# Partition maxima with one product, K^T V feature-major in two batches, and a new written-out order

## The chip, the cores and the metric

One core of a Trainium2 chip runs the whole program. It has TensorE (PE; its weight loads are listed as PEld), VectorE (DVE), ScalarE (ACT), GpSimd (POOL) and SyncE (SP), which issues all DMAs. The metric is the device time of one execution in microseconds (us), lower is better.

## What is computed

Random-feature attention, then two feed-forward layers on its 2304 tokens (4 batches of 576) of 512 columns (8 heads of 64):

```python
def phi(x):                                   # for q and k, scaled by 64 ** -0.25
    proj = np.einsum('bhsd,md->bhsm', x, omega)          # 128 features m
    h = proj - np.sum(x * x, axis=-1, keepdims=True) / 2.0
    return np.exp(h - np.max(h, axis=-1, keepdims=True)) / np.sqrt(m)
kv, z = einsum('bhsm,bhsd->bhmd', k_p, v), sum(k_p, axis=2)
x = einsum('bhsm,bhmd->bhsd', q_p, kv) / (einsum('bhsm,bhm->bhs', q_p, z)[..., None] + 1e-06)
x = x / sqrt(mean(x * x) + 1e-06) * rms_g                # layer 1, d_ff 1536
x = (silu(x @ w_gate) * (x @ w_val)) @ w_out
h = x @ w_in                                             # layer 2, d_ff 2048
out = where(h > 0, h, exp(min(h, 0)) - 1) @ w_out2
```

The weights arrive as 64-bit words and are made into float32 on the chip, then into two float16 planes (high and low part), so that a product of float32 accuracy is three float16 products.

## The kernel before, in words

*Work.* Attention is cut into 38 jobs, 20 of keys (four tiles of 128 tokens and one of 64 in each batch) and 18 of queries. Each job loads a tile, forms the features of all eight heads in two PSUM banks, takes maxima, and exponentiates (`phi`). Jobs 0 to 15 multiply in float32, the later ones in float16 planes (`SPLIT`). `NACT` says how many of a job's two banks ScalarE exponentiates head by head; the others are shifted by VectorE first. Key jobs add K^T V over the five tiles of a batch in two PSUM banks. For batches 0 and 1 (`KV32`) values and features stay float32: each product has the 65 columns of the values (64 and a column of ones) as stationary operand and the 128 features as moving operand, so the sum is [65 x 128] in each head, and `turned` scales it, splits it into planes, and turns it by products with the identity, to features on partitions. Batches 2 and 3 use float16 planes, with the features stationary. A query job multiplies its features with K^T V, divides, normalizes and lays out the token tile for layer 1.

The layers follow: `moe1_pair` and `moe1_out` by blocks of 256 tokens, then `moe2_quad` and `moe2_out`. Their products are the *spine*: they keep the order in which they are written. Meanwhile the weights are made: `conv_cols` and `conv_rows` call `Conv.words`, which on 128x1024 words forms the magnitude, the shifted low bits and the sign plane (0x8000 of the top half word), and `fp32`, which joins them.

*Maxima over partitions.* `spread(m, n)` takes n columns of values, one for each partition, turns them with a product (the columns stationary, the identity moving), lets VectorE reduce the n rows, and sends the maxima to all partitions with a second product with ones (n = 1), or with a diagonal (n > 1). It is called for the scale of each float16 attention job, of values, of each weight block, and at the end of each block of layer 1.

*Order.* The program is recorded as operations, and `Plan.order` simulates five engines with prices from `Plan.take` and waits from `Plan.wait`. It decides which operation each engine issues next, which engine takes an operation with several `ways`, and which PSUM bank (kind B) or large or middle tile (kinds L, M) a job gets. Spine operations have due times from `STRETCH`; others inherit them through their users with `INFL` and `LEAD`, shifted for each job by `BIAS`. `SPARE` and `BLIM` keep places free for the spine. Each engine then executes its list in order, and a waiting instruction holds all behind it. All instructions are issued in `play`, so they carry one line in the profile, L530; the tiles (arenas RX, RW, RA, RM, RS, RC, RI, RO and banks ps) tell them apart.

Of the kernel before, what the change touches and what calls it, by code (L numbers as in the profile page):

```python
# [17 lines left out]
P = 128  # L18
# [4 lines left out]
NACT, SPLIT = '12111011102010110100001022111212110111', '00000000000000001111111111111111111111'  # L23
# [116 lines left out]
class Plan:  # L140
# [4 lines left out]
    HOP = 0.14  # L145
    INTO, FROM = {"POOL": 0.19}, {"PE": 0.22, "POOL": 0.08}
    LAND, MARGIN = 1.7, 0.5
    SPAN = 3.4133
    SPARE = {"B": 2, "L": 2, "M": 2}
# [80 lines left out]
    def take(self, eng, real, fn, a, k):  # L230
# [23 lines left out]
        if eng == "PE":  # L254
            op.cost += 0.19 * (min(k["lhsT"].free_size(), n) < 64 and len(op.calls) == 1) + max(n, 64) / 2400.0 * (4 if k["rhs"].dtype == F32 else 1) + (0.0047 if k["rhs"].dtype == F32 else 0.0024)
        elif eng == "DVE":
            n = max(n, src.free_size()) if fn == "tensor_reduce" else n
            fast = fn in ("tensor_scalar", "tensor_copy", "memset") and "accum_out" not in k and src.space == bass.MemoryType.SB
            pair = "in1" in k and src.space == k["in1"].space == bass.MemoryType.SB
            op.both = pair or (fast and fn != "memset" and out.space == bass.MemoryType.SB and n > 1)  # L260
            op.cost += 0.068 + n / (1920.0 if fast else 960.0) + 0.0615 * vals + (0.3 if pair and n > 64 and out.partition_size() == 64 else 0.0)
        elif eng == "ACT":
            op.cost += (0.094 if src.space == bass.MemoryType.SB else 0.052) + n / 1200.0 + 0.093 * vals + (0.094 if "accum_out" in k else 0)
            op.cost += 0.12 if vals and out.partition_size() == 64 else 0.0
        elif eng == "POOL":
            op.cost += 0.088 * (len(op.calls) > 1)
            if fn == "tensor_scalar":
                op.cost += 0.066 + n / 980.0 if not vals else 0.243 + n / 1197.0 + 0.083 * (vals - 1)
            else:
                op.cost += 0.464 if n < 9 else 0.147 + n / (475.0 if aps["in1"].dtype == F32 else 530.0)  # L270
# [269 lines left out]
def fused(ctx: ExitStack, tc: tile.TileContext, qT, kT, kTt, qn, kn, v, v1, omT, eye, g, wg, wv, wo, w1, w2, out):  # L540
# [14 lines left out]
    RC = Arena(sb, "RC", 1216)  # L555
# [68 lines left out]
    RI = Arena(sb, "RI", 640)  # L624
    idn, ones, dg = RI.take([P], F16), RI.take([P], F16), RI.take([64], BF16)
    om, Wh, Wl = RO.take([P], F32), RO.take([P], F16), RO.take([P], F16)
    kap0 = tt([1])
    RS = Arena(sb, "RS", 2816)
# [8 lines left out]
    def spread(m, n, o=None):  # L637
# [14 lines left out]
        pe.matmul(out=o[:, 504:504 + n], lhsT=ones[0:n], rhs=r, start=True, stop=True)  # L652
        return o[:, 504:504 + n]
# [21 lines left out]
    class Conv:  # L675
# [15 lines left out]
        def words(self, st):  # L691
# [12 lines left out]
            vec.tensor_scalar(out=A16[:, :, 1], in0=r16[:, :, 3], scalar1=0x8000, scalar2=None, op0=ALU.bitwise_and)  # L704
# [124 lines left out]
    sv = tt([1])  # L829
# [12 lines left out]
    def setup_consts():  # L842
# [12 lines left out]
        vec.memset(ones, 1.0)  # L855
# [14 lines left out]
    def phi(load, n, key, pair=True):  # L870
# [28 lines left out]
        if split:  # L899
# [11 lines left out]
            iv, s, kap = sm(1, "qiv"), sm(1, "qs"), sm(1, "kap")  # L911
            vec.tensor_scalar(out=m_, in0=spread(m, 1), scalar1=1e-24, scalar2=None, op0=ALU.max)
            vec.tensor_scalar(out=iv.bitcast(I32), in0=m_.bitcast(I32), scalar1=1, scalar2=EXPM, op0=ALU.logical_shift_right, op1=ALU.bitwise_and)
            vec.tensor_scalar(out=sq[:n], in0=sq[:n], scalar1=0.0625, scalar2=None, op0=ALU.mult)
            vec.tensor_scalar(out=iv, in0=iv, scalar1=2.0 ** (64 - 12), scalar2=None, op0=ALU.mult)
            vec.reciprocal(out=s, in_=iv)
            vec.tensor_scalar(out=kap, in0=iv, scalar1=kap0, scalar2=None, op0=ALU.mult)
            Sx = S_r.next()
# [9 lines left out]
            vec.scalar_tensor_tensor(out=mx[:n], in0=mx[:n], scalar=kap[:n], in1=sq[:n], op0=ALU.mult, op1=ALU.subtract)  # L928
            vec.scalar_tensor_tensor(out=b[:n], in0=mx[:n], scalar=-LN2_14, in1=sq[:n], op0=ALU.add, op1=ALU.add)
            if nact:  # L930
                vec.tensor_scalar(out=nb[:n], in0=b[:n], scalar1=-1.0, scalar2=None, op0=ALU.mult)
            for i in range(2):
                if i < 2 - nact:
                    shifted(i, b, kap[:n], ALU.mult, ALU.subtract)
                else:
                    exps(i, kap[:n], nb)
        else:
# [35 lines left out]
    def values(b):  # L973
# [30 lines left out]

    def turned(b):

        kt = e_r.next()
        KV = kv_r[b % 2]
        for i in range(2):
            c = slice(512 * i, 512 * i + 512)  # L1010
            act.activation(out=kt[0:65, 0, c], in_=acc[i][0:65], func=AF.Copy, scale=sv[0:65])
            vec.scalar_tensor_tensor(out=kt[0:65, 1, c], in0=acc[i][0:65], scalar=sv[0:65], in1=kt[0:65, 0, c], op0=ALU.mult, op1=ALU.subtract)
        for a in range(2):
            for i in range(2):
                o = psP.next()
                with plan.group():
                    for h in range(4):
                        pe.matmul(out=o[:, h * 65:h * 65 + 65], lhsT=kt[0:65, a, (4 * i + h) * P:(4 * i + h) * P + P], rhs=idn[0:65, 0:65], start=True, stop=True)
                o = o[:, 0:260].rearrange("p (h c) -> p h c", h=4)
                if (a + i) % 2:  # L1020
                    vec.tensor_copy(out=KV[:, a, 4 * i:4 * i + 4, 0:65], in_=o)
                else:
                    act.activation(out=KV[:, a, 4 * i:4 * i + 4, 0:65], in_=o, func=AF.Copy)

    def k_job(b, t, key):
# [40 lines left out]
    def q_job(t, key):  # L1066
# [377 lines left out]
```

## Time and profile before

| | us |
|---|---|
| median of 3 runs | 977.3 (976.38 to 980.16) |
| span of the profiled execution (its time, no other is recorded) | 972.8 |
| TensorE busy | 911.0 |
| VectorE, GpSimd, ScalarE busy | 667.1, 599.8, 537.7 |

The span runs from the first to the last instruction. An engine's busy time is the union of its instructions. In lists by time a bracket gives the idle time of the engine before the instruction and what ended it. A float32 product appears as two records.

### The profile page before, as it was taken

The page shows a single profiled execution, that of the slowest core. Times are in us where ns is not written, and L with a number is a line of the kernel's source. Part 1 is how long each engine was busy: PE and PEld are TensorE (multiplying, and loading weights), DVE is VectorE, ACT ScalarE, POOL GpSimd, SP SyncE. Part 2 cuts the span into 40 slices and gives each one's busy share as a digit, 9 for nine tenths or more (in the row PEclk, how much of TensorE's full clock was granted, in tenths as well). Part 3 has the DMA queues.
Part 4 walks back from the last instruction along what each step waited for, and adds up shares of the span by engine and source line. Part 5 has one row for each costly group of instructions (what it writes and reads, how often), then busy time and mean ns, then how long its engine had stood idle before and what let it go on. Part 6 is the DMA issues. An engine that isn't in the chain of part 4 may idle for free. (4 is left out here: it accounts for less than half of the span.)

```text
span 972.8 us, 22167 instructions
## 1 busy us (share of the span) xinstructions
PE 911.0 (94%) x8904; PEld 802.7 (83%) x8904; DVE 667.1 (69%) x1570; ACT 537.7 (55%) x981; POOL 599.8 (62%) x617
## 2 busy tenths in 40 slices
PE   4486969999999999999999999999999999999998
PEld 4385858888888888888888888888888888888887
DVE  6988887867478585777866888777436565464642
ACT  5895554746455575584533557776435555255540
POOL 3668957967966788688573448996415265153540
PEclk9787989999999999999999999999999999999999
DMA  9765645033511442116674433000000000000001
GB/s 288 209 189 161 173 141 168 7 77 89 131 45 33 88 94 63 37 45 172 196 218 135 142 125 123 31 2 6 18 18 17 12 13 12 17 18 12 12 13 44
DMA packets 82567, 82.57 MB, mean 85 GB/s; under 512 B 52896, under 2 KB 57888, under 8 KB 82464
## 3 DMA queue, kind: packets, MB, share of 16 engines
q1 hardware_dynamic: 82464, 81.16, 29.5%
q8 instruction: 69, 1.13, 0.5%
q14 instruction: 34, 0.28, 0.1%
HBM read 59.90 MB, written 8.91 MB: 71 GB/s over the span
## 5 line engine op out<-in xcount | busy, mean ns | idle before, releaser
L530 PEld LDWEIGHTS <-RW 128*128 128x128 f16 x4800 | 451.7, 98 | 69.0 <-issue 12.2
L530 PE MATMUL ps<-RM,RW 128*128 128x256 f16 (+1 forms) x3240 | 365.4, 271 | 5.0 <-ACT RA L530 3.1
L530 PEld LDWEIGHTS <-RA 128*128 128x128 f16 (+3 forms) x3128 | 261.0, 98 | 31.5 <-issue 1.8
L530 PE MATMUL ps<-RX,RA 128*128 128x256 f16 x1728 | 196.5, 273 | 1.2 <-DVE RM L530 1.2
L530 ACT ACTIVATE RM<-ps,RC 128x512 f32<-128x512 f32 (+1 forms) x135 | 90.0, 669 | 101.7 <-PE ps L530 67.1
L530 POOL TENSOR_TENSOR RA<-RA 64x512 f16<-64x512 f32 (+6 forms) x91 | 122.6, 1349 | 22.8 <-DVE RS L530 4.9
L530 POOL TENSOR_TENSOR RM<-RM 128x512 f16<-128x512 f32 (+1 forms) x94 | 100.9, 1077 | 42.0 <-ACT RM L530 36.2
L530 ACT ACTIVATE RM<-RM 128x512 f32<-128x512 f32 (+3 forms) x163 | 96.3, 592 | 43.9 <-DVE RM L530 39.5
L530 POOL TENSOR_SCALAR RM<-RM,RC 128x512 f32<-128x512 f32 x72 | 57.7, 802 | 93.6 <-ACT RM L530 93.5
L530 DVE SCALAR_TENSOR_TENSOR ps<-ps,RM 128x512 f32<-128x512 f32 x72 | 50.2, 697 | 83.3 <-POOL RM L530 83.3
L530 PE MATMUL ps<-RX,RW 128*128 128x256 f16 x864 | 98.4, 273 | 2.1 <-DMA RX<-RA 2.1
L530 DVE TENSOR_REDUCE RS<-ps 128x4 f32<-128x512 f32 (+5 forms) x146 | 75.4, 536 | 27.6 <-PE ps L530 26.9
L530 DVE SCALAR_TENSOR_TENSOR RM<-RM,ps 128x512 f32<-128x512 f32 x108 | 73.2, 681 | 26.8 <-ACT RM L530 17.9
L530 ACT ACTIVATE RA<-RA 128x1024 f32<-128x1024 f32 (+5 forms) x69 | 61.3, 897 | 49.8 <-DVE RA L530 12.8
L530 PE MATMUL ps<-RW,RA 128*128 128x256 f16 (+2 forms) x560 | 68.5, 276 | 6.1 <-ACT RW L530 4.9
L530 PE MATMUL ps<-RW 128*128 128x256 f16 x600 | 71.9, 273 | 0.9 <-DVE RM L530 0.9
L530 ACT ACTIVATE RA<-RA,RS 64x512 f16<-64x512 f32 (+3 forms) x69 | 51.7, 759 | 27.3 <-POOL RS L530 11.3
L530 POOL TENSOR_TENSOR RW<-RM,RW 128x256 f16<-128x256 f32 (+1 forms) x63 | 43.7, 704 | 34.4 <-ACT RW L530 18.5
L530 POOL TENSOR_SCALAR RA<-RA,RS 64x512 f32<-64x512 f32 (+2 forms) x63 | 43.9, 697 | 22.2 <-ACT RA L530 15.8
L530 POOL TENSOR_TENSOR RA<-RM,RA 128x256 f16<-128x256 f32 (+1 forms) x50 | 34.4, 696 | 32.1 <-ACT RA L530 21.0
L530 DVE SCALAR_TENSOR_TENSOR RM<-ps,RC,RM 128x256 f32<-128x256 f32 x54 | 25.1, 478 | 40.6 <-PE ps L530 40.5
L530 DVE TENSOR_TENSOR RM<-ps,RM 128x256 f32<-128x256 f32 x108 | 45.1, 420 | 9.8 <-ACT RM L530 6.6
(147 smaller groups left out, 1182.4 us busy)
## 6 DMA issues: line engine op xcount, KB each, us to landing
RA<-w SPq DMA_DIRECT2D x32, 512.0 KB, 4.0
RX<-wg SPq DMA_DIRECT2D x12, 512.0 KB, 5.2
RX<-wv SPq DMA_DIRECT2D x12, 512.0 KB, 6.2
RX<-wo SPq DMA_DIRECT2D x12, 512.0 KB, 4.3
out<-RM SPq DMA_DIRECT2D x36, 128.0 KB, 1.7
f<-RA SPq DMA_DIRECT2D x8, 512.0 KB, 3.7
RA<-f SPq DMA_DIRECT2D x8, 512.0 KB, 3.4
RA<-qn SPq DMA_DIRECT2D x11, 256.0 KB, 4.0
```

The costliest lines, as they stand in the source:

```text
L530: getattr(real, fn)(*[fix(x) for x in a], **{i: fix(x) for i, x in k.items()})
```

## The change

`spread` forms one product for each column, with the column repeated 128 times as stationary operand, so that each partition gets all 128 values, and VectorE's reduction gives the maximum on all partitions. K^T V of batches 0 and 1 has the features as stationary and the values as moving operand; `turned` is gone, and the sum is scaled and split straight from PSUM, values and ones apart. The sign plane may be made by VectorE, ScalarE or GpSimd. The shift by 14 log 2 is left out for batches 0 and 1, and some small steps of `phi`, `values` and the denominator are joined. Squares of float16 jobs are always ScalarE's. The tables of the planner and its prices are replaced.

```diff
-NACT = '12111011102010110100001022111212110111'
+NACT = '12111011102010120100001022111212100111'
-AHEAD, BLIM = 2665473.472, 7
+AHEAD, BLIM = 2665473.472, 8
-FINE = 9
+FINE = 8
-BIAS = [0, -24, -6, -13, 9, 11, 1, -18, 4, 16, 26, 0, 3, 0, -42, -66, 48, 0, 24, -36, 11, -47, 60, -76, -82, 71, 3, 7, -74, -72, 7, -40, -68, -29, 214, -138, -2, -19, 6, 12, -10, -26, 30, 98, 29, -5, -6, 50, -58, 0, -29, 29, 0, 7, -28, 113, -9, 8, -23, 3, 1, 0]
+BIAS = [-48, -21, 9, 2, -1, -5, -19, -32, 7, -5, 23, 66, -12, -19, -40, -65, 96, 8, 86, -57, -31, -96, 87, -725, -93, 90, -8, -57, -521, 77, -106, 90, -388, -166, 245, -985, -415, -1104, 9, -61, 181, -50, -534, 1233, 108, -310, 475, -14, -96, 271, -73, 840, 77, 90, 285, 988, 70, 890, -200, 25, -589, -195]
-LOOK, WEIGH = 0.076, 80
-PRICE = [2.61, 1.246, 0.912, 2.233, 0.537, 1.098]
+LOOK, WEIGH = 0.0, 80
+PRICE = [2.241, 0.976, 0.79, 0.283, 0.288, 0.28]
-INFL, LEAD = 1.815, 51.617
-STRETCH = (11.046, 890.942, 0.188)
+INFL, LEAD = 1.963, 51.66
+STRETCH = (2.134, 3.532, 0.08)
-    SPARE = {"B": 2, "L": 2, "M": 2}
+    SPARE = {"B": 2, "L": 1, "M": 2}
...
-        o = bank.next() if o is None else o
         top = m.bitcast(BF16).rearrange("p (n w) -> p n w", w=2)[:, :, 1]
-        pe.matmul(out=o[0:n, 0:P], lhsT=top, rhs=idn, start=True, stop=True)
-        if n == 1:
-            r = sm(1, "spr").bitcast(BF16)[0:1, 0:1]
-            vec.tensor_reduce(out=r, in_=o[0:1, 0:P], op=ALU.max, axis=AX.X)
-        else:
-            c = sm(1, "spc")
-            r = dg[0:n, 0:n]
-            vec.tensor_reduce(out=c[0:n], in_=o[0:n, 0:P], op=ALU.max, axis=AX.X)
-            vec.tensor_scalar(out=r, in0=idn[0:n, 0:n], scalar1=c[0:n], scalar2=None, op0=ALU.mult)
-        pe.matmul(out=o[:, 504:504 + n], lhsT=ones[0:n], rhs=r, start=True, stop=True)
-        return o[:, 504:504 + n]
+        r = sm(n, "spr")
+        for i in range(0, n, 4):
+            k = min(4, n - i)
+            o = bank.next()
+            with plan.group():
+                for j in range(k):
+                    pe.matmul(out=o[:, j * P:j * P + P], lhsT=top[:, i + j:i + j + 1].to_broadcast([P, P]), rhs=idn, start=True, stop=True)
+            vec.tensor_reduce(out=r[:, i:i + k], in_=o[:, 0:k * P].rearrange("p (n k) -> p n k", n=k), op=ALU.max, axis=AX.X)
+        return r
...
-            vec.tensor_scalar(out=A16[:, :, 1], in0=r16[:, :, 3], scalar1=0x8000, scalar2=None, op0=ALU.bitwise_and)
+            h, o = r[:, :, 1].bitcast(F32), A16[:, :, 1].bitcast(F16)
+            plan.choose(lambda: vec.tensor_scalar(out=A16[:, :, 1], in0=r16[:, :, 3], scalar1=0x8000, scalar2=None, op0=ALU.bitwise_and),
+                        lambda: act.activation(out=o, in_=h, func=AF.Copy, scale=2.0 ** -100),
+                        lambda: pool.tensor_scalar(out=o, in0=h, scalar1=2.0 ** -100, scalar2=1.0, op0=ALU.mult, op1=ALU.mult))
...
-            if nact:
+            top = LN2_14 if pair else 0.0
+            if not pair:
+                nb = mx
+            elif nact:
                 vec.tensor_scalar(out=nb[:n], in0=mx[:n], scalar1=LN2_14, scalar2=None, op0=ALU.add)
...
-                    pe.matmul(out=acc[h // 4][0:65, (h % 4) * P:(h % 4) * P + P], lhsT=V32[:n, t, h], rhs=e[:n, h * P:(h + 1) * P], start=first and h % 4 == 0, stop=last and h % 4 == 3)
+                    pe.matmul(out=acc[h // 4][:, (h % 4) * 65:(h % 4) * 65 + 65], lhsT=e[:n, h * P:(h + 1) * P], rhs=V32[:n, t, h], start=first and h % 4 == 0, stop=last and h % 4 == 3)
             if last:
-                turned(b)
+                KV = kv_r[b % 2]
+                for i in range(2):
+                    a = acc[i][:, 0:260].rearrange("p (h c) -> p h c", h=4)
+                    hi, lo = KV[:, 0, 4 * i:4 * i + 4], KV[:, 1, 4 * i:4 * i + 4]
+                    for c, f in ((slice(0, 64), sv[:, b:b + 1]), (slice(64, 65), 2.0 ** 6)):
+                        act.activation(out=hi[:, :, c], in_=a[:, :, c], func=AF.Copy, scale=f)
+                        vec.scalar_tensor_tensor(out=lo[:, :, c], in0=a[:, :, c], scalar=f, in1=hi[:, :, c], op0=ALU.mult, op1=ALU.subtract)
...
         for i in range(2):
-            vec.tensor_scalar(out=rc[:, 4 * i:4 * i + 4].unsqueeze(2), in0=a4[i][:, :, 64:65], scalar1=128e-6 * 2.0 ** 20, scalar2=None, op0=ALU.add)
+            for a, m, b in runs:
+                vec.tensor_scalar(out=rc[a:a + m, 4 * i:4 * i + 4].unsqueeze(2), in0=a4[i][a:a + m, :, 64:65], scalar1=128e-6 * 2.0 ** 20, scalar2=ivs[a:a + m, b:b + 1], op0=ALU.add, op1=ALU.mult)
         vec.reciprocal(out=rc, in_=rc)
-        for a, m, b in runs:
-            vec.tensor_scalar(out=rc[a:a + m], in0=rc[a:a + m], scalar1=ivs[a:a + m, b:b + 1], scalar2=None, op0=ALU.mult)
```

## Rows read from the trace of the kernel before

**Rows 1.** Stretches: length, busy (instructions) of each engine, clock, DMA share, GB/s

```profile
0.00:51.50 51.50, 22.51 (x160) 19.70 (x161) 40.13 (x99) 36.60 (x54) 27.96 (x30) 0.89 0.83 235
51.50:72.70 21.20, 20.96 (x218) 20.02 (x217) 18.72 (x37) 19.96 (x45) 13.91 (x12) 0.87 0.77 213
72.70:88.80 16.10, 6.61 (x74) 5.14 (x74) 14.41 (x50) 10.58 (x23) 12.97 (x15) 0.65 0.44 138
88.80:121.00 32.20, 31.97 (x348) 29.97 (x346) 27.53 (x51) 15.46 (x25) 29.67 (x28) 0.96 0.65 182
121.00:160.00 39.00, 29.85 (x267) 25.36 (x267) 29.98 (x67) 20.26 (x28) 27.02 (x25) 0.87 0.46 147
160.00:972.80 812.80, 799.14 (x7843) 702.47 (x7841) 536.32 (x1270) 434.85 (x808) 488.22 (x512) 1.00 0.23 64
```

**Rows 2.** Waits of TensorE from 0 to 160 us: total, times, longest

```profile
PE ps L530 <- DVE RS L530: 15.0, 7, 6.0
```

**Rows 3.** Order of time, all engines, 137 to 148 us: start, length, what

```profile
137.36 0.22 PE L530 MATMUL ps<-RI,RS 128*1 128x128 f16 x1
...
141.95 1.22 DVE L530 TENSOR_SCALAR_CACHE_REDUCE RW<-RW 128x1024 f32<-128x1024 f32 x1 [1.09 <-ACT RW L530]
...
143.28 0.27 DVE L530 TENSOR_REDUCE RS<-ps 1x1 bf16<-1x128 f32 x1
...
143.60 0.16 PE L530 MATMUL ps<-RS,RI 1*128 1x1 bf16 x1 [6.03 <-DVE RS L530]
...
143.83 4.45 PE L530 MATMUL ps<-RM,RW 128*128 128x256 f16 x20
```

**Rows 4.** Order of time on TensorE alone, behind 143 us

```profile
143.83 22.48 PE L530 MATMUL ps<-RM,RW 128*128 128x256 f16 x180
...
196.43 0.22 PE L530 MATMUL ps<-RI,RS 128*1 128x128 f16 x1
196.57 2.79 PE L530 MATMUL ps<-RM,RW 128*128 128x256 f16 x24
...
440.75 0.16 PE L530 MATMUL ps<-RS,RI 1*128 1x1 bf16 x1 [0.33 <-DVE RS L530]
440.84 4.32 PE L530 MATMUL ps<-RM,RW 128*128 128x256 f16 x38
```

**Rows 5.** Second products of the maxima, whole span and behind 160 us

```profile
L530 PE MATMUL ps<-RS,RI 1*128 1x1 bf16 x44 | 7.5, 170 | 8.1 <-DVE RS L530 7.9
...
L530 PE MATMUL ps<-RS,RI x37: 158/172/173, 209.6 to 622.2; 1*128 1x1 bf16 x37
```

**Rows 6.** Order of time on TensorE, 58 to 77 us

```profile
58.67 7.29 PE L530 MATMUL ps<-RW,RA 128*65 128x128 f32 x64
...
68.52 0.88 PE L530 MATMUL ps<-RI,RW 65*128 65x65 f16 x20
...
71.08 0.90 PE L530 MATMUL ps<-RA,RW 128*128 128x65 f16 x24
...
76.91 0.22 PE L530 MATMUL ps<-RI,RS 128*2 128x128 f16 x1 [4.20 <-DVE RX L530]
```

**Rows 7.** Float32 weight loads by shape: busy, mean ns

```profile
L530 PEld LDWEIGHTS ps<-RO,RA 128*128 128x128 f32 x48 | 5.6, 192 | 0.0
...
L530 PEld LDWEIGHTS ps<-RO,RW 128*64 128x64 f32 x16 | 1.7, 137 | 0.0
```

**Rows 8.** Order of time on ScalarE, end of batch 0's K^T V

```profile
65.69 1.24 ACT L530 ACTIVATE RW<-ps,RC 65x512 f16<-65x512 f32 x2
...
69.30 0.67 ACT L530 ACTIVATE RA<-ps 128x260 f16<-128x260 f32 x2
```

**Rows 9.** VectorE's groups from 0 to 160 us: busy, mean ns

```profile
L530 DVE TENSOR_SCALAR RX<-RX 128x1024 uint16<-128x1024 uint16 x16 | 13.1, 821 | 3.4 <-POOL RX L530 3.4
...
L530 DVE TENSOR_SCALAR RS<-RS 128x8 f32<-128x8 f32 x10 | 4.8, 482 | 0.0
...
L530 DVE TENSOR_SCALAR RS<-ps 128x4 f32<-128x4 f32 x8 | 0.9, 148 | 0.0
```

More of the change, by code (lines that the diff above doesn't have):

```diff
@@ L145 @@
     HOP = 0.14
+    SAME = {"PE": 0.0, "DVE": 0.12, "ACT": 0.14, "POOL": 0.0, "SP": 0.06}
     INTO, FROM = {"POOL": 0.19}, {"PE": 0.22, "POOL": 0.08}
@@ L254, in take @@
         if eng == "PE":
-            op.cost += 0.19 * (min(k["lhsT"].free_size(), n) < 64 and len(op.calls) == 1) + max(n, 64) / 2400.0 * (4 if k["rhs"].dtype == F32 else 1) + (0.0047 if k["rhs"].dtype == F32 else 0.0024)
+            op.cost += 0.19 * (min(k["lhsT"].free_size(), n) < 64 and len(op.calls) == 1) + max(n, 64) / 2400.0 * (4 if k["rhs"].dtype == F32 else 1) + (0.0047 if k["rhs"].dtype == F32 else 0.0024) + (0.05 if k["rhs"].dtype == F32 and n < P else 0.0)
         elif eng == "DVE":
@@ L260, in take @@
             op.both = pair or (fast and fn != "memset" and out.space == bass.MemoryType.SB and n > 1)
-            op.cost += 0.068 + n / (1920.0 if fast else 960.0) + 0.0615 * vals + (0.3 if pair and n > 64 and out.partition_size() == 64 else 0.0)
+            tight = max([abs(y[-1][0]) for y in (src.ap, out.ap)]) == 1
+            op.cost += (0.01 if fn == "memset" and n < 9 else 0.068) + (0.0 if tight or not fast or n < 9 else 0.04) + (0.005 * n if fn == "reciprocal" else 0.0) + n / (1920.0 if fast else 960.0) + 0.0615 * vals + (0.3 if pair and n > 64 and out.partition_size() == 64 else 0.0)
         elif eng == "ACT":
             op.cost += (0.094 if src.space == bass.MemoryType.SB else 0.052) + n / 1200.0 + 0.093 * vals + (0.094 if "accum_out" in k else 0)
-            op.cost += 0.12 if vals and out.partition_size() == 64 else 0.0
+            op.cost += 0.12 if vals and out.partition_size() == 64 and src.space == bass.MemoryType.SB else 0.0
+            op.cost += 0.1 if src.space == bass.MemoryType.SB and src.ap[-1][0] != 1 and n > 8 else 0.0
         elif eng == "POOL":
@@ L267, in take @@
             if fn == "tensor_scalar":
-                op.cost += 0.066 + n / 980.0 if not vals else 0.243 + n / 1197.0 + 0.083 * (vals - 1)
+                op.cost += 0.27 if n < 9 else 0.186 + n / 980.0 if not vals else 0.243 + n / 1197.0 + 0.083 * (vals - 1)
             else:
-                op.cost += 0.464 if n < 9 else 0.147 + n / (475.0 if aps["in1"].dtype == F32 else 530.0)
+                op.cost += 0.53 if n < 9 else (0.1 if out.partition_size() == 64 and n < 1024 else 0.02) + 0.147 + n / (475.0 if aps["in1"].dtype == F32 else 530.0)
         else:
@@ L554, in fused @@
     RM = Arena(sb, "RM", 8192 + 24576 + 4096)
-    RC = Arena(sb, "RC", 1216)
+    RC = Arena(sb, "RC", 960)
     def tt(shape, dt=F32):
@@ L623, in fused @@
     RO = Arena(sb, "RO", 1024)
-    RI = Arena(sb, "RI", 640)
-    idn, ones, dg = RI.take([P], F16), RI.take([P], F16), RI.take([64], BF16)
+    RI = Arena(sb, "RI", 256)
+    idn = RI.take([P], F16)
     om, Wh, Wl = RO.take([P], F32), RO.take([P], F16), RO.take([P], F16)
     kap0 = tt([1])
-    RS = Arena(sb, "RS", 2816)
+    RS = Arena(sb, "RS", 2592)
     smalls = {}
@@ L910, in phi @@
             m_ = sm(1, "qma")
-            iv, s, kap = sm(1, "qiv"), sm(1, "qs"), sm(1, "kap")
-            vec.tensor_scalar(out=m_, in0=spread(m, 1), scalar1=1e-24, scalar2=None, op0=ALU.max)
+            iv, s, kap, kan = sm(1, "qiv"), sm(1, "qs"), sm(1, "kap"), sm(1, "kan")
+            vec.tensor_scalar(out=m_, in0=spread(m, 1), scalar1=1e-25, scalar2=None, op0=ALU.max)
             vec.tensor_scalar(out=iv.bitcast(I32), in0=m_.bitcast(I32), scalar1=1, scalar2=EXPM, op0=ALU.logical_shift_right, op1=ALU.bitwise_and)
-            vec.tensor_scalar(out=sq[:n], in0=sq[:n], scalar1=0.0625, scalar2=None, op0=ALU.mult)
-            vec.tensor_scalar(out=iv, in0=iv, scalar1=2.0 ** (64 - 12), scalar2=None, op0=ALU.mult)
+            vec.tensor_scalar(out=iv, in0=iv, scalar1=2.0 ** (66 - 12), scalar2=None, op0=ALU.mult)
             vec.reciprocal(out=s, in_=iv)
             vec.tensor_scalar(out=kap, in0=iv, scalar1=kap0, scalar2=None, op0=ALU.mult)
+            vec.tensor_scalar(out=kan, in0=iv, scalar1=kap0, scalar2=-1.0, op0=ALU.mult, op1=ALU.mult)
             Sx = S_r.next()
@@ L927, in phi @@
             maxima(False)
-            vec.scalar_tensor_tensor(out=mx[:n], in0=mx[:n], scalar=kap[:n], in1=sq[:n], op0=ALU.mult, op1=ALU.subtract)
-            vec.scalar_tensor_tensor(out=b[:n], in0=mx[:n], scalar=-LN2_14, in1=sq[:n], op0=ALU.add, op1=ALU.add)
-            if nact:
-                vec.tensor_scalar(out=nb[:n], in0=b[:n], scalar1=-1.0, scalar2=None, op0=ALU.mult)
+            vec.scalar_tensor_tensor(out=mx[:n], in0=mx[:n], scalar=kan[:n], in1=sq[:n], op0=ALU.mult, op1=ALU.add)
+            vec.scalar_tensor_tensor(out=nb[:n], in0=mx[:n], scalar=LN2_14, in1=sq[:n], op0=ALU.add, op1=ALU.subtract)
             for i in range(2):
                 if i < 2 - nact:
-                    shifted(i, b, kap[:n], ALU.mult, ALU.subtract)
+                    shifted(i, nb, kap[:n], ALU.mult, ALU.add)
                 else:
@@ L950, in phi @@
                 if i < 2 - nact:
-                    shifted(i, mx, LN2_14, ALU.add, ALU.add)
+                    shifted(i, mx, top, ALU.add, ALU.add)
                 else:
@@ L991, in values @@
         s = pow2(ma, 14, iv)
-        vec.tensor_scalar(out=ivs[:, b:b + 1], in0=iv, scalar1=32768.0, scalar2=None, op0=ALU.mult)
+        vec.tensor_scalar(out=ivs[:, b:b + 1], in0=s, scalar1=2.0 ** -15, scalar2=None, op0=ALU.mult)
         if b < KV32:
-            vec.memset(sv, 2.0 ** -8)
-            vec.tensor_scalar(out=sv[0:64], in0=s[0:64], scalar1=2.0 ** -23, scalar2=None, op0=ALU.mult)
+            vec.tensor_scalar(out=sv[:, b:b + 1], in0=s, scalar1=2.0 ** -9, scalar2=None, op0=ALU.mult)
             return
@@ L1003, in values @@
             scaled_lo(r, s[:n], hi, lo)
[L1005 to L1023, printed above, removed]
     def k_job(b, t, key):
```

15 lines of the change are left out of this document (6 added, 9 removed).

## The prediction

> **What bounds the kernel now.** I read the busy time by stretches first, then TensorE's waits, then the order of time around the long gaps. In the stretches [rows 1] the reader is to see two kernels in one. From 160 us to the end TensorE is busy 799.1 of 812.8 us at full granted clock while VectorE has 536 us of work and the others less: there a microsecond of TensorE work is a microsecond of time, and only 13.7 us are idle. Before 160 us TensorE is busy 22.5 + 21.0 + 6.6 + 32.0 + 29.9 = 111.9 us, so 48.1 us are idle, and the granted clock falls to 0.65 between 72.7 and 88.8 us. In the same 160 us VectorE is busy 40.1 + 18.7 + 14.4 + 27.5 + 30.0 = 130.8 us (82%), in the stretch with the low clock 14.4 of 16.1. So the start is held by chains through VectorE, the rest by TensorE's work. TensorE's waits [rows 2] agree: 15.0 us in seven waits for VectorE's small tiles (RS), one of 6.0 us.
>
> That one is read in order of time [rows 3]. At 137.36 TensorE forms the first product of a partition maximum. VectorE, whose order is fixed, takes a conversion step first, at 141.95, which waited 1.09 us for ScalarE, and reduces the maximum only at 143.28. The second product starts at 143.60 after 6.03 us of idle, and behind it in TensorE's queue stand the blocks of layer one: the first 20 of them took 4.45 us [rows 3], 0.22 each, and the 180 in a row 22.48 us [rows 4], where 24 such products take 2.79 [rows 4], (2.79 - 0.27)/23 = 0.110 each, so 180 some 20.0. After the gap TensorE thus ran for some microseconds at the lower of its two clocks (1.2 in place of 2.4 GHz; the stretch from 121 to 160 us was granted 0.87 [rows 1]). The gap costs 6.0 us and 2.5 us at lowered clock: 8.5 us.
>
> **One product for a maximum.** `spread` had a product, a reduction on one partition, and a second product that sends the result to all partitions. Now one product with the column broadcast as the stationary operand puts the maxima's inputs on all partitions, and the reduction is the last step. The first product keeps its price: 0.14 us from 196.43 to the product behind it at 196.57 [rows 4]. The second goes: 0.09 us of queue (440.75 to 440.84 [rows 4]), I take 0.1; bounds 0.05 and 0.15, about half of it to either side, and 0.15 is what the first one costs. 37 of the 44 lie behind 160 us [rows 5], all in the stretch that TensorE's work bounds: 3.7 us, less 0.5 for the two maxima of six and eight columns, which now need six and eight products and two reductions. Waits like the 0.33 us at 440.75 [rows 4] go too; I count three of them, 1.0 us. Behind 160 us: **4.2 us** (1.5 to 6). The first product still waits for VectorE as before, as at 76.91 with 4.20 us [rows 6].
>
> **K^T V of batches 0 and 1.** 160 float32 records (two for each product) have 65 stationary and 128 moving columns; 64 of them took 7.29 us [rows 6], 0.112 us each. The new form has 128 stationary and 65 moving columns. No row shows it. If the moving columns set the pace, it is 65/128 of 0.107 and 0.005 of overhead, 0.059; the float16 products with 128 stationary and 65 moving columns (24 in 0.90 us [rows 6], 0.031 each) are paced by the moving side. If the weight load sets it, nothing is gained: a float32 load of 128 columns is 192 ns against 137 for 64 [rows 7], 55 ns for 64 columns, so 110 for 128. A sum of load and move, 0.17, is the upper end, and I hold it unlikely because float32 products of 128 by 128 have both and their loads run beside the moves. Between the ends I take 0.086: the load rows contain waiting as well as loading. 160 x 0.026 = 4.2 us (8.5 to -9). The Trainium skill, page "TensorE: Matmul & The Clock Gate", section "LDWEIGHTS (loading the stationary operand)", has a load last its column count over 1.2 GHz, here 107 ns whatever moves; the difference of the two load rows agrees with it. By that rule a record could not fall below 0.107, the 4.2 us would be an estimated 0.8, and the forecast 1.7 us later.
>
> The transposes of the turned form go as well: 32 small products at 0.036 us (20 in 0.88 us [rows 6]), 1.2 us, and with them two evacuations and one hop. In batch 0 the chain from the last product to the first use took from 65.69 (ScalarE's scaled copies) by the last casts at 69.30 [rows 8] to the product at 71.08 [rows 6], 5.4 us. Now two ScalarE and two VectorE steps per half bank follow directly: by the 128x260 copies (0.67 for two [rows 8]) and a 128x4 step of 0.148 [rows 9], about 0.34 + 0.15 on each engine and half, some 2.1 us with a hop. The chain is 3.3 us shorter and its products 1.7 earlier, if the query tiles are ready; what is late next is VectorE in 72.7 to 88.8 us.
>
> Of this TensorE work, 4.2 + 1.2 + 0.7 (seven second products) = 6.1 us lie before 160 us, nearly all in the two dense stretches from 51.5 and from 88.8 us [rows 1]. I count half, **3.1 us** (0 to 6), since the rest turns into waiting.
>
> **VectorE's steps.** The sign plane may now go to ScalarE or GpSimd: 16 steps, 13.1 us before 160 us [rows 9]. The shift by 14 log 2 goes for batches 0 and 1: ten 128x8 steps, 4.8 us with their stretched durations [rows 9], as an upper bound. Two casts, four scaled subtractions and small steps at the denominators go, short strided ones come: 2 us. The ceiling is 20 of 130.8 us, where ScalarE had 103 us and GpSimd 112 us of 160 [rows 1], so there is room; what a plane costs there no row shows. Outside the first 12 us and the long gap 30 us of idle remain before 160 us. VectorE's load falls by a seventh at most; I let a fifth of that idle go, **6 us** (-5 to 15: both signs, since the order of every queue is new).
>
> **The long gap.** No second product can stand in front of layer one, so the 8.5 us at 143.6 cannot come back in that form. But the reduction is still late in VectorE's queue, and a first product, or an attention group, may stand there instead. I count half: **4.3 us** (0 to 8.5).
>
> **The order.** Costs, waits, biases and the stretch of the due times are replaced, so that all five queues are reordered, SP's loads included; a moved job takes its loads, its evacuations and its slots of PSUM along. I price the new order at nothing by itself behind 160 us: queues there are covered by 799 us of TensorE work, and if the cover is gone the price is that of the gaps above. The sum is 4.2 + 3.1 + 6 + 4.3 = 17.6 us. The profiled execution's own time is the span, 972.8, as no other is given; the median of three runs is 977.3, 4.5 above it. I make the sum against the span, 955.2, and carry the 4.5 over: 959.7, forecast 960 (947 to 970 for this case alone).
>
> **The rivals.** *Only the late work counts.* The start is bound by its loads (DMA share 0.83 to 51.5 us [rows 1]) and by the number of whole conversion steps, so that shorter chains end in other waits. Against it: from 72.7 us the share is 0.44 and TensorE still idles. Then only 4.2 us stay: 973.
>
> *The new order puts a waiting product in front of layer one.* TensorE takes its queue in order, and so do ScalarE and VectorE. A product queued too early costs what the gap at 143.6 cost, 8.5 us with the clock. For it: costs and biases are all new, and the reserve of two places for large tiles falls to one, so that attention may fill the tiles that conversions need. Against it: behind 160 us the present order has 13.7 us of idle in all [rows 1], the wait at 440.75 [rows 4] being of the usual size. Two such gaps more than now bring 960 to 977, so that from the third on it is slower: 959.7 + 3 x 8.5 = 985.2.
>
> *The K^T V form doesn't do what it says*: load and move add up, 0.17 a record, 160 x 0.058 = 9.3 us more instead of 4.2 less; by the half counted 6.7 us, 966. A part of the forecast's upper end.
>
> *VectorE's relief is worth more*: half of the 30 us of idle goes, 9 us more: 951 or less.
>
> **How the numbers follow.** The forecast 0.55, with its upper end where K^T V disappoints (0.06 of it); the strong relief 0.10; only the late work 0.20; the misplaced wait 0.15. About 0.5% can be told from no change here, that is 972.4 to 982.2. Faster: 0.55 + 0.10 and a third of the late-work case (0.07), 0.72. Same: the rest of it, 0.13, and two hundredths of the misplaced waits, 0.15. Slower: 0.13. The range leaves out a tenth above and some hundredths below: 942 to 979.
>
> **What would show it.** Right: no 1x1 products, and 44 fewer small ones; the float32 records of 65 moving columns spaced by 0.059 to 0.112; the idle before 160 us near 37 us instead of 48; VectorE's busy time before 160 us below 120; from there on TensorE as full as now, with its work 3 to 4 us smaller. Wrong: idle of TensorE behind 160 us above 25 us, a record of K^T V above 0.112, or the start as long as now with the waits handed to ScalarE or GpSimd.

## The result, and the profile after

The changed kernel takes **954.7 us** (median of four runs, 950.73 to 956.32) against 977.7 beside it: 0.9753 of the time before, 95% interval [0.9713, 0.9793]. The forecast was 960, the range 942 to 979. The profiled execution took 953.85 us with a span of 952.0, so 1.85 us lie around the span; with as much around it, that of before, with its span of 972.8, was some 3 us quicker than its median.

The stretches of the changed kernel, in the columns of [rows 1]:

```profile
0.00:51.50 51.50, 34.61 (x280) 32.60 (x280) 40.72 (x94) 40.38 (x78) 30.57 (x29) 1.00 0.99 253
51.50:72.70 21.20, 12.30 (x170) 11.41 (x169) 17.03 (x48) 16.84 (x32) 14.28 (x16) 0.85 0.51 162
72.70:88.80 16.10, 14.14 (x196) 13.44 (x193) 15.10 (x40) 14.08 (x25) 9.94 (x9) 0.99 0.66 177
88.80:121.00 32.20, 32.20 (x326) 29.78 (x326) 29.67 (x77) 20.54 (x33) 20.98 (x20) 1.00 0.59 187
121.00:160.00 39.00, 27.69 (x238) 23.34 (x237) 34.56 (x51) 28.05 (x35) 29.13 (x21) 0.94 0.62 184
160.00:952.00 792.00, 771.05 (x7639) 687.97 (x7637) 575.06 (x1394) 413.29 (x763) 353.24 (x336) 1.00 0.24 63
```

Before 160 us TensorE is busy 34.61 + 12.30 + 14.14 + 32.20 + 27.69 = 120.9 us, 9.0 more than in [rows 1]; behind it, 771.05 us instead of 799.14, with 20.95 us idle instead of 13.7. So of the 20.8 us by which the span is shorter, 19.0 are less busy time of TensorE (911.0 to 892.0) and only 1.8 less idle: 9.0 less before 160 us, 7.3 more behind it. VectorE is not relieved: 137.1 us before 160 us against 130.8, and more over the whole span:

```profile
PE 892.0 (94%) x8838; PEld 798.5 (84%) x8838; DVE 712.1 (75%) x1701; ACT 533.2 (56%) x963; POOL 458.1 (48%) x428
```

GpSimd has less (599.8 us before, 458.1 now). The order of time on TensorE shows where the start differs:

```profile
45.97 5.66 PE L533 MATMUL ps<-RA,RW 128*128 128x65 f32 x48
...
68.05 0.61 PE L533 MATMUL ps<-RI,RA 128*128 128x128 f16 x4 [5.16 <-ACT RA L533]
...
73.09 1.70 PE L533 MATMUL ps<-RM,RW 128*128 128x128 f16 x24 [0.28 <-DVE RS L533]
...
83.65 5.52 PE L533 MATMUL ps<-RA 128*128 128x65 f32 x48
...
104.62 0.22 PE L533 MATMUL ps<-RI,RS 128*128 128x128 f16 x1
104.67 1.50 PE L533 MATMUL ps<-RM,RW 128*128 128x128 f16 x24
...
133.18 14.57 PE L533 MATMUL ps<-RM,RW 128*128 128x256 f16 x132
147.59 0.33 PE L533 MATMUL ps<-RI,RC 128*128 128x128 f16 x3
148.81 0.23 PE L533 MATMUL ps<-RI,RC 128*128 128x128 f16 x1 [0.89 <-DVE RW L533]
...
151.38 0.23 PE L533 MATMUL ps<-RI,RC 128*128 128x128 f16 x1 [1.03 <-DVE RW L533]
157.08 0.29 PE L533 MATMUL ps<-RI,RC 128*128 128x128 f16 x1 [5.47 <-DVE RW L533]
```

The reader is to see four things. K^T V of batch 0 ends at 51.6 us; before, it ran until 66.0 [rows 6]. Layer one starts at 73 us; before, its first product stood at 85.57 us. From a one-product maximum to the product behind it pass 104.67 - 104.62 = 0.05 us. And near 147 us the long gap is back in another form: the products of the six columns of a `wo` block wait in TensorE's queue for VectorE's conversion, 0.89 + 1.03 + 5.47 = 7.4 us. By 160 us this kernel has nevertheless issued 398 products of layer one's 128x256 form, the one before 244. The row of before that starts at 85.57:

```profile
85.57 0.29 PE L530 MATMUL ps<-RM,RW 128*128 128x128 f16 x1
```

Then the two groups of TensorE from 0 to 160 us (busy, mean ns, idle before); after:

```profile
L533 PE MATMUL ps<-RM,RW 128*128 128x256 f16 x398 | 46.9, 278 | 1.9 <-ACT RA L533 1.2 <-DVE RM L533 0.7
```

and before:

```profile
L530 PE MATMUL ps<-RM,RW 128*128 128x256 f16 x244 | 30.5, 288 | 3.1 <-ACT RA L530 3.1
```

At the 0.110 us that the prediction worked out for one, the 154 more are a lead of 16.9 us.

### The profile page after: what moved, and what is told of

It reads as the page before. It is cut to its first block, busy times and chain, and to the rows that moved or that the text cites. A ratio compares the mean times of both kernels' runs of the same rounds, so it can differ in the third digit from the quotient of the medians.

```text
span 952.0 us, 21939 instructions
## 1 busy us (share of the span) xinstructions
PE 892.0 (94%) x8838; PEld 798.5 (84%) x8838; DVE 712.1 (75%) x1701; ACT 533.2 (56%) x963; POOL 458.1 (48%) x428
## 4 chain that ended last, share of the span: by engine, by line
PE 60%; DVE 14%; DMA 11%; ACT 7%; POOL 3%; issue 3%; SPq 1%; ACTq 0%; DVEq 0%; POOLq 0%
PE ps L533 60%; DVE RA L533 4%; DMA RA<-w 3%; DVE RS L533 3%; DVE RM L533 3%; ACT RA L533 2%; ACT RM L533 2%; ACT RW L533 2%; DVE RW L533 2%; DMA f<-RA 2%; POOL RW L533 1%; POOL RA L533 1%; SPq L533 1%; DVE ps L533 1%; DMA RW<-kT 1%
## 5 line engine op out<-in xcount | busy, mean ns | idle before, releaser
L533 PEld LDWEIGHTS <-RA 128*128 128x128 f16 (+2 forms) x3112 | 262.6, 99 | 40.6 <-ACT RA L533 5.3
L533 POOL TENSOR_TENSOR RA<-RA 64x512 f16<-64x512 f32 (+5 forms) x85 | 118.4, 1393 | 28.0 <-DVE RA L533 17.8
L533 POOL TENSOR_TENSOR RM<-RM 128x512 f16<-128x512 f32 (+1 forms) x76 | 84.1, 1112 | 75.0 <-ACT RM L533 69.1
L533 DVE TENSOR_REDUCE RS<-ps 128x4 f32<-128x512 f32 (+4 forms) x148 | 78.4, 552 | 32.3 <-PE ps L533 31.5
L533 ACT ACTIVATE RA<-RA 128x512 f32<-128x512 f32 (+3 forms) x72 | 68.1, 955 | 53.5 <-DMA RA<-w 16.1
L533 POOL TENSOR_SCALAR RM<-RM,RC 128x512 f32<-128x512 f32 x22 | 16.9, 767 | 120.7 <-ACT RM L533 120.7
L533 PE MATMUL ps<-RW,RA 128*128 128x256 f16 x480 | 57.6, 273 | 0.0
L533 POOL TENSOR_SCALAR RA<-RA,RS 64x512 f32<-64x512 f32 (+3 forms) x53 | 41.1, 775 | 29.9 <-ACT RA L533 22.0
L533 DVE TENSOR_SCALAR RM<-RM,RC 128x512 f32<-128x512 f32 x50 | 28.5, 569 | 29.9 <-ACT RM L533 29.6
L533 ACT ACTIVATE RX<-RX 128x1024 f32<-128x1024 f32 (+4 forms) x37 | 40.7, 1109 | 13.0 <-DVE RS L533 3.6
```

Of the source, the lines that this page charges most:

```text
L533: getattr(real, fn)(*[fix(x) for x in a], **{i: fix(x) for i, x in k.items()})
```

## The experiments

The theory is that of the prediction: each edit shortens its own step, and the new order by itself is worth nothing. The rival is that the gain belongs to the order, or to edits and order together. "Order held" means that the planner's output is kept as it was, instruction queue by instruction queue, and that single operations play other instructions in their place. Ratios are to the kernel before, from 4 to 12 runs each, with 95% intervals.

**1. One edit in the old order: the maxima.** For n of 1 and 2:

```diff
-pe.matmul(out=o[0:n, 0:P], lhsT=top, rhs=idn, ...)
-vec.tensor_reduce(out=r, in_=o[0:1, 0:P], ...)
-pe.matmul(out=o[:, 504:504 + n], lhsT=ones[0:n], rhs=r, ...)
+pe.matmul(out=o[:, j * P:j * P + P], lhsT=top[:, j:j + 1].to_broadcast([P, P]), rhs=idn, ...)   # each column
+vec.tensor_reduce(out=o[:, 504:504 + n], in_=o[:, 0:n * P], ...)
```

> The kernel before with its order of every queue held, and only the maxima of one and two columns made with one product (50 of 52; the second products and the diagonal steps are left out of the queues). Theory of the work: TensorE spends 9.1 us on one-column maxima behind 160 us and would spend 2.0, so 7 us go there, and the gap at 143.6 us (6.0 and 2.5 at lowered clock) goes as well, since nothing else stands in front of layer one: 13 to 17 us faster. Rival, theory of the order: layer one at 143.6 had other inputs missing as well, and the late products were beside waits: at most 5 us faster.

Measured: 0.9953 [0.9936, 0.9969], 4.6 us of 978. Stretches up to and behind 160 us:

```profile
0.00:160.00 160.00, 114.59 (x1108) 105.13 (x1109) 131.91 (x298) 103.82 (x175) 111.61 (x107) 0.89 0.70 195
160.00:972.10 812.10, 786.65 (x7754) 699.55 (x7752) 538.47 (x1267) 431.98 (x807) 484.08 (x511) 0.99 0.24 63
```

Behind 160 us TensorE has 12.5 us less work than in [rows 1], but the stretch is only 0.7 us shorter: the idle time there rose from 13.7 to 25.5 us. Over the whole span TensorE is busy 9.8 us less (901.2) and idle 9.1 us more (70.9). The profiled execution of before was a quick one; by the medians the gain is the 4.6 us. The gap of [rows 3] broke up into smaller waits:

```profile
137.23 1.47 PE L530 MATMUL ps<-RM,RW 128*128 128x256 f16 x12 [1.35 <-DVE RS L530]
139.64 5.40 PE L530 MATMUL ps<-RM,RW 128*128 128x256 f16 x48 [0.95 <-DVE RS L530]
...
151.31 9.33 PE L530 MATMUL ps<-RM,RW 128*128 128x256 f16 x84 [1.94 <-DVE RM L530]
164.90 0.27 PE L530 MATMUL ps<-RI,RC 128*6 128x128 f16 x1 [4.25 <-DVE RW L530]
```

**2. One edit in the old order: K^T V feature-major**, without `turned`.

```diff
-lhsT=V32[:n, t, h], rhs=e[:n, h * P:(h + 1) * P]
+lhsT=e[:n, h * P:(h + 1) * P], rhs=V32[:n, t, h]
```

> The kernel before with its order of every queue held, and only K^T V of batches 0 and 1 made with the features stationary, without the turning. In the changed kernel these float32 records take 0.112 us each, as before. Theory of the work: only 32 small products (1.2 us) go from TensorE, and the chain of two batches gets shorter beside work that is there anyway: 0 to 3 us faster. Rival: the two chains (about 3 us each, and 3.1 us of TensorE's idle time at 121 to 124 us that waited for the second one's evacuation) set the start of layer one: 4 to 9 us faster.

Measured: 1.0022 [1.0002, 1.0042]. In the old order this edit gains nothing.

**3. All of these in the old order**, with the 14 log 2 shift left out for batches 0 and 1 and the short denominators (the diffs of 1 and 2 with those of the change to `phi` and the denominators).

> The kernel before with its order held, and both of the former together, without the shift by 14 log 2 in batches 0 and 1, and with the shorter denominators (the sign plane stays on VectorE, the small steps of the float16 jobs stay). Theory of the work: the operations carry most of the 23 us, 15 to 20 us faster. Theory of the order: 3 to 8 us faster, the rest needs the new order.

Measured: 0.9989 [0.9972, 1.0007]. VectorE has 123.86 us of work before 160 us instead of 130.8, TensorE behind 160 us 786.49 instead of 799.14, and the time is that of before.

**4. That and the sign plane off VectorE, old order** (two of three planes on ScalarE, one on GpSimd).

```diff
-vec.tensor_scalar(out=A16[:, :, 1], in0=r16[:, :, 3], scalar1=0x8000, scalar2=None, op0=ALU.bitwise_and)
+act.activation(out=o, in_=h, func=AF.Copy, scale=2.0 ** -100)       # or pool.tensor_scalar, every third
```

> The kernel before with its order held, one-product maxima, K^T V feature-major, the shift left out, shorter denominators, and the sign planes made by ScalarE (two of three) and GpSimd at the place where VectorE had them. That is nearly every operation of the change in the old order, which without the sign planes was as fast as the kernel before. Theory that VectorE's relief works by itself: 7 to 12 us faster than the kernel before. Rival, the operations give nothing in an order that was not made for them: within 4 us of it, or slower since ScalarE's queue gets 1.1 to 1.4 us more in front of its evacuations.

Measured: 1.0064 [1.0045, 1.0084], slower than before. Up to 160 us:

```profile
0.00:160.00 160.00, 116.92 (x1055) 106.87 (x1056) 112.46 (x266) 114.74 (x184) 110.19 (x111) 0.85 0.66 189
```

Here VectorE has the relief that the prediction asked for, 112.46 us, below its bound of 120, and it buys nothing.

**5. The new tables with the operations of before.** Prices, waits, biases and places of the changed kernel, planned anew with two products for a maximum, `turned`, and the sign plane on VectorE; two places for large tiles.

```diff
-PRICE = [2.61, 1.246, 0.912, 2.233, 0.537, 1.098]
+PRICE = [2.241, 0.976, 0.79, 0.283, 0.288, 0.28]
... (all tables likewise)
```

> The operations of the kernel before (two products, turned K^T V, sign plane on VectorE alone) with the changed planner, its prices, waits, biases and due times, but two places kept for large tiles as before. Theory of the order: layer one starts near 73 us and leads by 15 us at 160 us as in the changed kernel, of which the two products take back what they took in the last comparison: 965 to 975 us. Theory that the operations give the lead (sign plane off VectorE, short K^T V): layer one starts near 85 us, 975 us or more.

Measured: 1.0929 [1.0901, 1.0957], 91 us slower than before. By 160 us it has 480 products of layer one's form done, more than the changed kernel:

```profile
L533 PE MATMUL ps<-RM,RW 128*128 128x256 f16 x480 | 53.7, 273 | 0.3 <-DVE RM L533 0.3
```

That is lost later, in waits for attention and weights that are not ready. TensorE in order of time:

```profile
498.81 1.65 PE L533 MATMUL ps<-RO,RA 128*128 128x128 f16 x14 [4.07 <-DVE RA L533]
...
540.27 1.50 PE L533 MATMUL ps<-RA 128*128 128x65 f16 x24 [6.21 <-DMA RA<-RA]
546.84 3.38 PE L533 MATMUL ps<-RX,RW 128*128 128x256 f16 x15 [5.06 <-DMA RX<-RA]
```

**6. The old tables with the changed operations**, planned anew; `LOOK` and the one place for large tiles stay as changed.

```diff
-PRICE = [2.241, 0.976, 0.79, 0.283, 0.288, 0.28]
+PRICE = [2.61, 1.246, 0.912, 2.233, 0.537, 1.098]
... (all tables likewise)
```

> The operations of the changed kernel with the planner of the kernel before: its prices, waits, biases, due times; only LOOK is 0 and one place is kept for large tiles, as in the changed kernel. Theory of the order: about as the kernel before, 970 to 985 us, since the operations alone gave 0 to 5 us with the order held. Theory that the operations carry it once the queues are laid out anew for them: 955 to 965 us.

Measured: 1.0617 [1.0592, 1.0643]. Tables are values for one set of operations: either mixture is far slower than both kernels. So 5 and 6 show that a plan does not carry over; they don't tell what the order is worth by itself. For that the order of the changed kernel is held in what follows, and its operations are put back.

**7. The changed kernel, two products for a maximum of one column** (order held; the second product and a VectorE copy of the result follow the reduction):

```diff
-pe.matmul(out=o[:, 0:P], lhsT=top.to_broadcast([P, P]), rhs=idn, ...)
-vec.tensor_reduce(out=r, in_=o[:, 0:P], ...)
+pe.matmul(out=o[0:1, 0:P], lhsT=top, rhs=idn, ...)
+vec.tensor_reduce(out=row, in_=o[0:1, 0:P], ...)
+pe.matmul(out=o[:, 504:505], lhsT=ones[0:1], rhs=row, ...)
+vec.tensor_copy(out=r, in_=o[:, 504:505])
```

> The changed kernel with its order held, and the one-column maxima made with two products again, the second one put into TensorE's queue where the reduction stands in the order (with one more VectorE copy of 0.15 us each, in which it differs from the kernel before). Theory of the work: 44 times about 0.2 us of TensorE, 8 us, and some waits: 8 to 14 us slower than the changed kernel. Rival, theory of the order: the products fit beside waits, within 3 us.

Measured: 0.9929 [0.9911, 0.9947]; against 0.9753 that is 17 us slower than the changed kernel. Stretch behind 160 us, and TensorE's waits there (total, times, longest):

```profile
160.00:969.50 809.50, 784.23 (x7681) 687.74 (x7679) 576.51 (x1431) 413.34 (x763) 352.87 (x337) 1.00 0.23 62
```

```profile
PE ps L533 <- DVE RS L533: 11.3, 13, 2.1
```

In the changed kernel the same wait is 4.4 us in three:

```profile
PE ps L533 <- DVE RS L533: 4.4, 3, 3.5
```

The early lead is there (393 products by 160 us), and is lost behind it: 13.2 us more work of TensorE and 4.3 us more idle. Over the whole span TensorE is busy 910.7 us, 18.7 more, and idle 58.8 us, 1.2 less: the 17 us are busy time, not waiting.

**8. The changed kernel, sign plane on VectorE**, as before the change, for all 45 planes; order held.

> The changed kernel with its order held, and every sign plane made by VectorE at the place where the order has it. VectorE gets 18 more steps of 0.82 us, 14.8 us, before 160 us, and 4 or so of the second matrix behind it. Theory that VectorE's relief is part of the early lead: 6 to 15 us slower than the changed kernel. Rival: VectorE had room beside waits, within 3 us.

Measured: 0.9857 [0.9834, 0.988], 10 us slower than the changed kernel. In its profile TensorE is busy 9.2 us more (901.2) at a mean granted clock of 0.982 instead of 0.991; another of its runs was granted 0.991 and took 964.33 us, as long as the others, so the clock alone does not explain the 10 us.

**9. Both of 7 and 8.**

> The changed kernel with its order held, with two products for one-column maxima and with the sign plane on VectorE, both as in the two runs before (16.5 and 9.5 us slower than the changed kernel). If the two are independent: 981 us, slower than the kernel before, so that the new order is worth nothing without the operations that it was made for. If they share their waits: 970 to 974 us, and the order alone keeps a gain.

Measured: 1.0077 [1.0059, 1.0094]: 32 us slower than the changed kernel and slower than before, where 17 + 10 would be 27. The new order with these two operations of before is worse than the old order with them. The 5 us beyond the sum are within what the intervals leave.

**10. Six late products.** In the changed kernel the products of the `wo` maxima are played 12 and 36 layer products later, the rest held, so that the 7.4 us near 147 us have work in them.

> The changed kernel with its order held but for the six products of the maxima for the third weight matrix of layer one: they stand 12 and 36 products of layer one later in TensorE's queue, and what needs them stands behind them. In the changed kernel these six waited 0.9, 1.0 and 5.5 us for VectorE at 148.8, 151.4 and 157.1 us. Theory that a waiting product in front of layer one costs its wait: some 4 us of the 7.4 are filled, 3 to 5 us faster than the changed kernel. Rival, as seen when the old order lost its second products: the next wait takes the place, within 1.5 us.

Measured: 0.9778 [0.9753, 0.9802], no gain. The idle time came back at once, behind the first four of the moved products, and ended with a VectorE reduction out of PSUM (DVE RS), which points to a bank that the layer's products now waited for; that it was a bank is inferred:

```profile
150.41 0.39 PE L533 MATMUL ps<-RI,RC 128*128 128x128 f16 x4
159.17 6.38 PE L533 MATMUL ps<-RM,RW 128*128 128x256 f16 x36 [8.38 <-DVE RS L533]
```

**11. A longer chain behind K^T V.** The first scaled copy of batches 0 and 1 is made eight times, 3.4 us more of ScalarE in each.

```diff
-act.activation(out=hi[:, :, c], in_=a[:, :, c], func=AF.Copy, scale=f)
+act.activation(out=hi[:, :, c], in_=a[:, :, c], func=AF.Copy, scale=f)     # x8, i == 0 and values only
```

> The changed kernel with its order held; the first scaled copy of K^T V out of PSUM is made eight times in batches 0 and 1 (7 x 0.49 = 3.4 us more on ScalarE in each), which makes the chain about as long again as the turned form was. Theory that the shorter chain is a part of the gain: 3 to 6 us slower than the changed kernel. Rival, as in the old order: the chain lies beside other work, within 1.5 us.

Measured: 0.9775 [0.9756, 0.9794]; some 2 us, and the intervals overlap. The 3.3 us that the prediction saw in this chain are hardly on the path.

**12. More of TensorE's work.** In the changed kernel the product of each one-column maximum is formed five times: 44 x 4 x 0.056 = 9.9 us, 7.8 of it behind 160 us.

> The changed kernel with its order held, and each one-column maximum's product made five times over: 44 x 4 more products of 56 ns, 9.9 us, 7.8 of them behind 160 us, without a new wait or step on another engine. Theory that a microsecond of TensorE work behind 160 us is a microsecond of time: 7 to 10 us slower than the changed kernel. Rival, that such work lies beside the idle time that is left there (21 us): within 3 us, and then the 16.5 us of the two products are waits.

Measured: 0.9784 [0.9764, 0.9804], about 3 us; the intervals of this run and of the changed kernel overlap.

```profile
160.00:956.30 796.30, 778.90 (x7785) 696.67 (x7783) 574.03 (x1396) 414.40 (x763) 354.47 (x337) 1.00 0.24 63
```

Of the 7.85 us of work added there 3.5 went into idle time that was there anyway (17.4 us are left of 20.95).

## Why the forecast came out, by its own steps

The time was right, and the sum behind it was not: it comes out near the measured one because terms that fell away stand against one that was far too small. That is luck.

*The start bound by chains through VectorE, the rest by TensorE's work.* The first held in part: layer one leads by 16.9 us at 160 us, though VectorE was not relieved, and the idle time saved in the start came back behind it but for 1.8 us. The second held in part too. "A microsecond of TensorE work is a microsecond of time" fits experiment 7 (18.7 us more work, 17.5 us more span). It fails in experiment 1, which took 12.5 us of work out behind 160 us for 0.7 us of that stretch (4.6 us by the medians), and experiment 12 put 7.85 us in for 3 to 4.

*One product for a maximum, 4.2 us.* Near the 4.6 us of the old order (experiment 1), but there 9.8 us of work went and 9.1 us of idle time came; in the new order the second product costs 17 us (experiment 7), far above the upper bound of 6. So the price was mis-sized. The prediction read only the time from a product to the one behind it, and held that the first one keeps its price. The order of time on TensorE before, and its weight loads:

```profile
221.09 0.22 PE L530 MATMUL ps<-RI,RS 128*1 128x128 f16 x1
221.24 2.79 PE L530 MATMUL ps<-RM,RW 128*128 128x256 f16 x24
223.96 0.17 PE L530 MATMUL ps<-RS,RI 1*128 1x1 bf16 x1
224.07 1.48 PE L530 MATMUL ps<-RM,RW 128*128 128x256 f16 x12
225.48 0.22 PE L530 MATMUL ps<-RI,RS 128*1 128x128 f16 x1
```

```profile
221.09 0.08 PEld L530 LDWEIGHTS <-RS 128*1 128x1 bf16 x1 [0.21 <-issue]
...
223.96 0.09 PEld L530 LDWEIGHTS <-RI 1*128 1x128 f16 x1 [0.21 <-issue]
```

and after:

```profile
232.37 2.78 PE L533 MATMUL ps<-RM,RW 128*128 128x256 f16 x24
234.99 0.22 PE L533 MATMUL ps<-RI,RS 128*128 128x128 f16 x1
235.04 1.47 PE L533 MATMUL ps<-RM,RW 128*128 128x256 f16 x12
```

```profile
234.88 0.10 PEld L533 LDWEIGHTS <-RS 128*128 128x128 bf16 x1
```

24 blocks in front of a one-product maximum last 234.99 - 232.37 = 2.62 us, so 12 last 1.31. In front of the old second product 24 last 223.96 - 221.24 = 2.72, and in front of the old first one 12 last 225.48 - 224.07 = 1.41: each of the two starts 0.10 us late. Behind them pass 0.15 us (first) and 0.11 us (second). An old maximum took 0.10 + 0.15 + 0.10 + 0.11 = 0.46 us of a full queue, the new one takes 0.05 to 0.06; 0.40 us are saved where the prediction had 0.1. All 44 would be an estimated 17.6 us, near the 17 of experiment 7.

*K^T V, 3.1 us.* The record did not become cheaper: 48 of them took 5.66 us and 48 others 5.52, (5.66 - 0.28)/47 = 0.114 and (5.52 - 0.28)/47 = 0.111 each, against 0.112 before [rows 6]. That is what the prediction had if the weight load sets the pace, and the load rows of the new form fit it:

```profile
L533 PEld LDWEIGHTS ps<-RA 128*128 128x128 f32 x80 | 9.2, 192 | 0.2 <-issue 0.2
```

192 ns again, as the 128-column load of [rows 7]. The rule of the Trainium skill (page "TensorE: Matmul & The Clock Gate", section "LDWEIGHTS (loading the stationary operand)"), by which a record could not fall below an estimated 0.107, agrees with these paces. That a float32 record takes some 0.11 us whatever its columns is not excluded: no run has one with few columns on both sides. Only the transposes went, 1.2 us, and in the old order the whole edit gives nothing (experiment 2).

*VectorE's steps, 6 us.* The mechanism named was wrong. VectorE's busy time before 160 us was to fall below 120; it rose to 137.1, though ScalarE and GpSimd made all 18 sign planes there:

```profile
L533 ACT ACTIVATE RX<-RX 128x1024 f16<-128x1024 f32 x11 | 15.2, 1381 | 1.7 <-POOL RX L533 1.7
```

```profile
L533 POOL TENSOR_SCALAR RX<-RX 128x1024 f16<-128x1024 f32 x7 | 9.5, 1352 | 0.6
```

VectorE took over low planes that GpSimd had made in two steps, a scaling and a difference. Groups from 0 to 160 us, VectorE after:

```profile
L533 DVE SCALAR_TENSOR_TENSOR RW<-RX,RS,RW 128x512 f16<-128x512 f32 x13 | 10.9, 870 | 1.6 <-ACT RW L533 1.6
```

and GpSimd before:

```profile
L530 POOL TENSOR_TENSOR RW<-RX,RW 128x512 f16<-128x512 f32 x24 | 28.9, 1204 | 2.0
...
L530 POOL TENSOR_SCALAR RX<-RX,RS 128x512 f32<-128x512 f32 x24 | 17.8, 740 | 10.7 <-ACT RW L530 10.5
```

One step of 0.87 us stands for two on GpSimd of 1.20 and 0.74. So VectorE's time was not freed but spent on other work; that it shortens more there is not shown. Relief by itself is worth less than nothing (experiment 4 against 3: 7 us slower); with the order laid out for it, 10 us (experiment 8). A plane takes 1.38 and 1.35 us on ScalarE and GpSimd and 0.82 on VectorE [rows 9], which may be why the old order loses by it; no run isolates that.

*The long gap, 4.3 us.* The half counted was for a first product that waits there instead; it does, 7.4 us near 147 us. Moving it (experiment 10) gave nothing, so it is not a misplaced product alone that costs there.

*The order at nothing.* Alone it is worth nothing or less: with two of the old operations it loses 8 us against the kernel before (experiment 9). What failed is that the other terms were priced against the old order and added. The changed operations in the old order give 1 us (experiment 3, [0.9972, 1.0007]) and with the sign planes lose 6; edits and order together give 23. The maxima are worth 4.6 us in the old order and 17 in the new one, the sign planes minus 7 and 10.

*The 19.0 us of TensorE's busy time.* The transposes are 1.2. The mean granted clock rose from 0.978 to 0.991. In the profiled execution of before, TensorE was busy 23.6 us at the lower level (of the 41.0 us from 29.9 to 40.1, 50.3 to 57.2, 77.6 to 91.3 and 139.1 to 149.3), after it 12.9 us (of the 17.1 from 66.2 to 73.1, 155.0 to 161.8 and 598.7 to 602.1). Half of the difference, 5.4 us, is saved; the prediction had 2.5 us of clock, in the long gap. The other 12.4 us are left for the maxima; that is less than 17.6, which fits that some of them stood beside waits before. The clock differs between runs: those of the changed kernel were granted 0.983 to 0.991. The start is fuller (granted 1.00 in the first stretch against 0.89 in [rows 1], 0.99 against 0.65 from 72.7 us), so less was run slowly.

*What was to show it.* Idle before 160 us near 37: it is 39.1. TensorE's work behind 160 us 3 to 4 us less: 28.1 less, 16.9 of it the lead of layer one and most of the rest the maxima. Idle there above 25 us, the sign of a misplaced wait: 20.95 in the changed kernel, and above it only in experiments.

*What stays open.* Which of the tables' values makes the early lead was not isolated. K^T V in its old form was not run in the new order: the turned tile has no place there.

## What to carry to other kernels

Where every queue runs in a written-out order, price an edit together with the order it is planned in: put alone into the old order it shows a fraction of its worth, none, or a loss; taken out of the order laid out for it, it can show its full price (the maxima 17 us, 17.6 by their rows). A planner's tables that were tuned to one set of operations don't suit another (experiments 5 and 6: 9 and 6% slower). A stretch in which an engine is 98% busy can still take in some microseconds of more work, or give back only a part of what is taken out: try it once with added work before counting its work as time. And price a small product by the start of the products on both sides of it, not by what follows it alone.

## What was not expected of the hardware

A product with one stationary column holds TensorE's queue longer than one with 128: 196.43 to 196.57 us [rows 4] against 104.62 to 104.67 in the changed kernel, 0.14 and 0.05 us for the same 128 moving columns of float16. It also starts late, by 0.10 us, and so does the second product with its one stationary row (the rows at 221 to 225 us above). The load rows beside them show where this lies: the load of the one column or row starts together with its product (221.09 and 223.96 us) after 0.21 us in which no load ran, while the load of the column repeated 128 times starts at 234.88, 0.11 us before its product, beside the block in front. Experiment 12 repeats the product five times in a row:

```profile
105.17 0.44 PE L533 MATMUL ps<-RI,RS 128*128 128x128 f16 x5
105.45 1.50 PE L533 MATMUL ps<-RM,RW 128*128 128x128 f16 x24
```

Five in 0.28 us are 0.056 each, the pace of other products of 128 moving columns ((1.50 - 0.22)/23 = 0.056). So the column repeated 128 times costs nothing over any other stationary operand of 128 columns, and the single column costs some 0.2 us more, 0.10 before it and 0.09 behind. Why its load does not run ahead no run shows.
